# Soft-MoE over linear attention on one core: early loads joined, w loads reordered, one output chunk stored in uneven pieces

## The chip, the cores and the metric

The kernel runs on one core of a Trainium2 chip. The metric is the device time of one execution in microseconds. Before the change it is 172.59 us, the median of three runs (172.44 to 172.74).

## What is computed

The reference, cut to its core. q, k and v are 8 batches x 8 heads x 576 x 64 in float32; x has 4608 rows of 512; there are 8 experts of 4 slots, with w1 of 512 x 1024 and w2 of 1024 x 512 each.

```python
kv = np.einsum('bhsd,bhse->bhde', k, v)
out = np.einsum('bhsd,bhde->bhse', q, kv)
out = out / np.sqrt(np.mean(out * out, -1, keepdims=True) + 1e-06) * g_norm
x = out.transpose(0, 2, 1, 3).reshape(B * S, H * D)

logits = x @ phi
d = softmax(logits, axis=0)
slot_input = (d.T @ x).reshape(E, S_per_e, D)
for e in range(E):
    slot_out[e] = np.maximum(slot_input[e] @ w1[e], 0.0) @ w2[e]
c = softmax(logits, axis=1)
return c @ slot_out.reshape(n_slots, D)
```

## The kernel before

The kernel is written for five engines and records every instruction in an Order object, which then puts the semaphore waits in. All instructions are issued from its one line 204, so the rows of the profile are told apart by their tiles. The engines keep the order in which the code calls them.

The 4608 rows of x are worked on in 36 tiles of 128, T0 to T35; nine tiles belong to two batches. For each batch b, the class Kv makes the products of k and v (methods products and borders, 64x64 matmuls named "psum<-arena" in the trace), and slots turns them and writes them into a block matrix bds[b % 2] through ACT. The function products(T) then multiplies q by that matrix (matmuls "psum<-bd,arena", 128x192), with two PSUM tiles in turn; square(T) and evict(T) let ACT copy the result out, VectorE makes the mean squares, GpSimd scales. The table kv_steps (line 625) says behind which tile the steps 0, 1 and 2 of a batch stand: steps 0 and 1 are its products, step 2 is slots. Logits, a running maximum and the weighted sums of x by groups of six tiles follow along.

When all tiles are done, expert_h makes relu(slot_input @ w1) for eight experts, expert_y the products with w2 in two halves, combine the row softmax. gather and mix collect a half, and output(hf, k, f) makes one of twelve output chunks: matmuls "psum<-logits,part", then ACT and VectorE copy to the chunk's place in SBUF, of 128 partitions x 1536 floats (6144 B a partition).

All inputs, w and the outputs lie in one SBUF array, arena, of 160 KB a partition, whose regions are used again: KV_AT, Q_AT, W_AT and OUT_AT give the places. All DMAs go out on SyncE (SP) in program order, and one waits until the last reader of its place is done. The early loads (lines 320 to 327) go out at once: "first" (constants and half of kv of batch 0), the other half of kv0, q of batches 0 and 1, kv1 in two halves, the rest of q0, kv2, q1. kv3, kv4 and kv5 follow behind batch 0's products (lines 685 to 687); then loads_behind (line 330) issues one load behind each of the tiles 9, 18, 24 and 27, and load_w is called by hand further down. W_ROWS (line 40) says which units of w1 and w2 (16 KB a partition each, some in halves) one load takes; its order is also the order in DRAM.

OUT_ROWS (line 51) says which chunks a store takes: chunks 0 to 2, 3 to 5, 6 and 7, 8 to 11, each as one DMA of 128 rows once its last chunk is written:

```python
for row in OUT_ROWS:
    if row[-1] == n:
        nc.sync.dma_start(out[...].rearrange("o (p n) -> (o p) n", p=P), place(OUT_AT[row[0]], m))
```

Of the kernel before, what the change touches and what calls it, by code (L numbers as in the profile page):

```python
# [5 lines left out]
F32 = mybir.dt.float32  # L6
# [5 lines left out]
P = 128  # L12
# [15 lines left out]
TOK = 4608  # L28
# [4 lines left out]
KV_AT = (0, 36, 54, 0, 90, 126, 18, 54)  # L33
Q_AT = (18, 72, 108, 36)
# [4 lines left out]
}  # L39
W_ROWS = (  # L40
    (("w1", 0, None), ("w1", 1, None)),
    (("w1", 2, None), ("w1", 3, None)),
    (("w1", 4, None), ("w2", 2, 1), ("w2", 0, None), ("w2", 1, None)),
    (("w2", 2, 0), ("w1", 6, None), ("w1", 5, None)),
    (("w1", 7, None),),
    (("w2", 3, None), ("w2", 4, None)),
    (("w2", 5, None), ("w2", 6, None)),
# [1 line left out]
)  # L49
OUT_AT = (32, 38, 44, 104, 110, 116, 122, 128, 134, 140, 146, 152)  # L50
OUT_ROWS = ((0, 1, 2), (3, 4, 5), (6, 7), (8, 9, 10, 11))
SHARED = (5, 11)
HEAD = 144
SCRATCH = 1024
# [206 lines left out]
def row_length(row):  # L261
    return sum(UNIT if part is None else UNIT // 2 for _, _, part in row)


def soft_moe_linear_attention(nc, first_in, kv_in, q0_in, q1_in, kv4_in, kv5_in, t3_in, w_in, out):


    const = Const(nc)
# [9 lines left out]
    def place(at, n):  # L278
        return arena[:, HEAD + at * KB : HEAD + at * KB + n]

    def load_row(at, src):
        nc.sync.dma_start(place(at, src.shape[-1]), src)
# [14 lines left out]
    def homes(kind, u):  # L297
        at = W_AT[kind, u]
        if at is None:
            return [xflat[:, :UNIT]]  # L300
        return [place(a, UNIT // len(at)) for a in at]

    def load_w(kind, u, part=None):
        i = [row[0] for row in W_ROWS].index((kind, u, part))
        lo = sum(row_length(row) for row in W_ROWS[:i])
        n = row_length(W_ROWS[i])
        src = w_in[:, lo * P : (lo + n) * P].rearrange("o (p n) -> (o p) n", p=P)
        t = homes(kind, u)[part or 0]
        if n > t.shape[-1]:
            t = place(W_AT[kind, u][part or 0], n)  # L310
        nc.sync.dma_start(t, src)

    def w_block(kind, u, i):
# [4 lines left out]


    nc.sync.dma_start(arena[:, : HEAD + 2304], first_in)  # L320
    load_row(KV_AT[0] + 9, kv_in[0, :, 2304:])
    load_row(Q_AT[0], q0_in[:, :2048])
    load_row(KV_AT[1], kv_in[1, :, :2304])
    load_row(KV_AT[1] + 9, kv_in[1, :, 2304:])
    load_row(Q_AT[0] + 8, q0_in[:, 2048:])
    load_row(KV_AT[2], kv_in[2])
    load_row(Q_AT[1], q1_in)


    loads_behind = {  # L330
        9: lambda: load_row(KV_AT[6], t3_in),
        18: lambda: load_w("w1", 0),
        24: lambda: load_w("w1", 2),
        27: lambda: load_w("w1", 4),
    }

    nc.scalar.preload_act_table_set("natural_log_exp_and_others")
# [4 lines left out]
    nc.gpsimd.memset(ones, 1.0)  # L342
    zeros = const.tile([P, 256], BF16, name="zeros")
    nc.vector.memset(zeros, 0.0)
    eps = const.tile([P, 1], F32, name="eps")
    nc.gpsimd.memset(eps, EPS_RMS)
    sel32 = const.tile([P, NS], F32, name="sel32")
# [5 lines left out]
    for i in range(2):  # L353
        lo = 64 * i
# [22 lines left out]
    class Kv:  # L377
# [10 lines left out]
        def products(self, r):  # L388
            g, w = divmod(r, 2)
            main = kv_main(self.b, g).rearrange("p (r w c n) -> p r w c n", r=2, w=2, c=4)  # L390
            for c in range(4):
                for i in range(2):
                    lo = 64 * i
                    nc.tensor.matmul(
                        self.pkv[lo : lo + 64, w, g],
                        lhsT=main[:, w, 1, c, lo : lo + 64],
                        rhs=main[:, w, 0, c, lo : lo + 64],
                        start=c == 0 and (g == 0 or self.b == 0),
                        stop=False,
                    )  # L400
# [222 lines left out]
    first = {b: 9 * (b // 2) + 4 * (b % 2) for b in range(B)}  # L623
    kvs = {}
    kv_steps = {(b, i - 3): (i,) for b in range(2, B) for i in range(3)}
    kv_steps.update({(1, -2): (0,), (1, -1): (1, 2)})
    kv_steps.update({(6, i - 4): (i,) for i in range(3)})
    del kv_steps[6, -1]

# [12 lines left out]
    ends = {starts[s + 1] - 1: s for s in range(len(STAGES))}  # L642
# [7 lines left out]
    def fill(n, cols=256, home=None):  # L650

        if not n:
            return
        t = home if home is not None else ps.tile([P, 2, 512], F32, tag="o", name="fill", bufs=2)[:, 1]
        for i in range(n):
            nc.tensor.matmul(
                t[:, :cols].rearrange("p (a n) -> p a n", n=256),
                lhsT=zeros[:, :P],
                rhs=zeros.unsqueeze(1).to_broadcast([P, cols // 256, 256]),
                start=True,  # L660
                stop=True,
            )
# [14 lines left out]
    for g in range(2):  # L677
        kv = Kv(0, "o" if g else "kv", 2 if g else None)
# [3 lines left out]
        fill(1, cols=512)  # L682
        kv.slots((g,))
        fill(EARLY[1 + g], cols=512)
    load_row(KV_AT[3], kv_in[3])
    load_row(Q_AT[1] + 8, kv4_in)
    load_row(Q_AT[2], kv5_in)
    T_at, diag_at, pb_at, d_at, sums_at = {}, {}, {}, {}, {}
    for T in range(NT - 2):
# [3 lines left out]
        o = products(T)  # L693
# [137 lines left out]
    def expert_h(e):  # L831
        ph = ps.tile([P, 2, 512], F32, tag="m", name=f"ph{e}")[:, 0, :256]
        for c in range(4):
            for j in range(4):
                nc.tensor.matmul(
                    ph[32 * j : 32 * j + 32],
                    lhsT=sTe[:, (4 * e + c) * NS : (4 * e + c + 1) * NS],
                    rhs=w_block("w1", e, 4 * c + j),
                    start=c == 0,
                    stop=c == 3,  # L840
                )
        h = wk.tile([P, 256], F32, tag="part", name=f"h{e}", bufs=3)
        nc.scalar.activation(h, ph, AF.Relu, scale=rs)

        x = xts[(NT - 1 - e // 2) % NX].rearrange("p j n -> p (j n)")
        hTs[e] = x[:, e % 2 * 256 : e % 2 * 256 + 256].rearrange("p (c n) -> p c n", n=NS)
        nc.vector.transpose(out=hTs[e].rearrange("p c n -> p (c n)"), in_=h)
# [28 lines left out]
    def mix(hf):  # L876
# [2 lines left out]
            nc.tensor.matmul(pz[f], lhsT=sel.rearrange("p a n -> p (a n)"), rhs=ys[hf][f], start=True, stop=True)  # L879
        zs[hf] = halves(f"z{hf}", pz)  # L880

    def output(hf, k, f):
        z = zs[hf]
        n = (hf * NCH + k) * 2 + f
        at = OUT_AT[n]
        st = place(at, 4 * CT * NS).rearrange("p (a n) -> p a n", a=4)
        shared = n in SHARED
        for v in range(2):
            fourth = hf == 1 and (2 * n + v) % 4 == 3
            apart = shared and v == 1  # L890
            pots = [
                ps.tile([P, 2, 512], F32, tag="y" if y else "m", name=f"po{hf}_{k}_{f}_{v}_{i}", bufs=1 if y else None)
                for i, y in enumerate((False, fourth) if apart else (fourth,))
            ]
            for u in range(2):
                lo = 32 * (2 * v + u)
                po = pots[u if apart else 0]
                nc.tensor.matmul(
                    po[:, 0 if apart else u, : CT * NS].rearrange("p (g x) -> p g x", g=2),
                    lhsT=z[f][lo : lo + 32],  # L900
                    rhs=cT[k][lo : lo + 32],
                    start=True,
                    stop=True,
                )
            if apart:
                nc.vector.tensor_copy(out=st[:, 2], in_=pots[0][:, 0, : CT * NS])
                nc.scalar.copy(st[:, 3], pots[1][:, 0, : CT * NS])
            elif v == 0:
                nc.scalar.copy(st[:, 0:2], pots[0][:, :, : CT * NS])
            else:  # L910
                nc.vector.tensor_copy(out=st[:, 2:4], in_=pots[0][:, :, : CT * NS])
        for row in OUT_ROWS:
            if row[-1] == n:
                lo, m = row[0] * 4 * CT * NS, len(row) * 4 * CT * NS
                nc.sync.dma_start(
                    out[:, lo * P : (lo + m) * P].rearrange("o (p n) -> (o p) n", p=P), place(OUT_AT[row[0]], m)
                )

    expert_h(0)
    expert_h(1)  # L920
    load_w("w2", 3)
# [20 lines left out]
    chunks = [(k, f) for k in range(NCH) for f in range(2)]  # L942
# [20 lines left out]
def build_program():  # L963
    import concourse.bacc as bacc

    nc = bacc.Bacc("TRN2", target_bir_lowering=False, num_devices=1, dynamic_dma_scratch_size=SCRATCH)
    shapes = {
        "first": (P, HEAD + 2304), "kv": (4, P, TOK), "q0": (P, TOK), "q1": (P, 2048),
        "kv4": (P, 2560 + TOK), "kv5": (P, 2 * TOK), "t3": (P, 3 * TOK),
        "w": (1, 2 * NE * P * UNIT),  # L970
    }
    args = [nc.dram_tensor(f"in_{n}_dram", s, F32, kind="ExternalInput").ap() for n, s in shapes.items()]
    args.append(nc.dram_tensor("out_0_dram", (1, 4 * NCH * P * 4 * CT * NS), F32, kind="ExternalOutput").ap())
    order = Order(nc)
    soft_moe_linear_attention(order, *args)
    order.emit()
    return nc
# [58 lines left out]
```

## Time and profile before

| | |
|---|---|
| median of three runs | 172.59 us |
| the profiled execution: its time | 172.53 us |
| its span, first to last instruction | 171.2 us |
| PE busy (matmul) | 149.1 us, 87% |
| ACT, DVE, POOL busy | 88.9, 86.0, 57.2 us |
| moved by DMA | 71.67 MB, mean 419 GB/s |
| data queue, share of 16 DMA engines | 97.6% |
| chain that ended last, by engine | PE 47%, DMA 26%, ACT 12%, DVE 5% |

The span is what the rows count from; the execution's own time is 1.3 us longer. The DMA share is the mean over the core's 16 DMA engines, and it counts a packet in the stretch in which it starts, so that short stretches can show more than 1. The instruction queues (q8 and q14) are fetches of code, which run on the same 16 engines as the data queue q1.

### The profile page before, as it was taken

The page shows a single profiled execution, that of the slowest core. Times are in us where ns is not written, and L with a number is a line of the kernel's source. Part 1 is how long each engine was busy: PE and PEld are TensorE (multiplying, and loading weights), DVE is VectorE, ACT ScalarE, POOL GpSimd, SP SyncE. Part 2 cuts the span into 40 slices and gives each one's busy share as a digit, 9 for nine tenths or more (in the row PEclk, how much of TensorE's full clock was granted, in tenths as well). Part 3 has the DMA queues.
Part 4 walks back from the last instruction along what each step waited for, and adds up shares of the span by engine and source line. Part 5 has one row for each costly group of instructions (what it writes and reads, how often), then busy time and mean ns, then how long its engine had stood idle before and what let it go on. Part 6 is the DMA issues. An engine that isn't in the chain of part 4 may idle for free.

```text
span 171.2 us, 4497 instructions
## 1 busy us (share of the span) xinstructions
PE 149.1 (87%) x1975; PEld 108.1 (63%) x1975; DVE 86.0 (50%) x184; ACT 88.9 (52%) x230; POOL 57.2 (33%) x68
## 2 busy tenths in 40 slices
PE   7787897989999899999899999999999988989400
PEld 3467776979688888898797775455565444445100
DVE  1122156283677265763936798724897027137400
ACT  2037576786965887768849864203213025137400
POOL 6000708548356755466482579200000000000000
PEclk9999999999999999999999999999999999999965
DMA  5999999999999999999999999998999999999995
GB/s 192 416 422 433 439 415 437 472 421 474 417 413 458 430 426 430 406 404 452 433 492 419 431 429 389 434 450 354 436 478 387 461 390 421 439 396 439 406 459 241
DMA packets 3476, 71.67 MB, mean 419 GB/s; under 512 B 384, under 2 KB 384, under 8 KB 384
## 3 DMA queue, kind: packets, MB, share of 16 engines
q1 hardware_dynamic: 3456, 71.38, 97.6%
q8 instruction: 15, 0.25, 0.5%
q14 instruction: 5, 0.04, 0.1%
HBM read 61.94 MB, written 9.44 MB: 417 GB/s over the span
## 4 chain that ended last, share of the span: by engine, by line
PE 47%; DMA 26%; ACT 12%; DVE 5%; SPq 2%; issue 1%
PE psum L204 47%; DMA arena<-in_kv_dram 13%; DMA arena<-in_w_dram 13%; ACT bd L204 3%; ACT sq L204 3%; ACT xall L204 2%; SPq L204 2%; DVE logits L204 1%; ACT arena L204 1%; DVE ms L204 1%; ACT part L204 1%; ACT d L204 1%; ACT r L204 1%; DVE r L204 0%; DVE d L204 0%
## 5 line engine op out<-in xcount | busy, mean ns | idle before, releaser
L204 PE MATMUL psum<-bd,arena 128*128 128x192 f32 (+1 forms) x320 | 56.1, 335 | 1.9 <-ACT bd L204 1.5
L204 PEld LDWEIGHTS psum<-bd,arena 128*128 128x128 f32 (+1 forms) x320 | 45.4, 179 | 7.1 <-ACT bd L204 2.8
L204 DVE TENSOR_REDUCE ms<-sq 128x16 f32<-128x1024 f32 (+1 forms) x19 | 22.1, 1162 | 32.6 <-ACT sq L204 32.3
L204 POOL TENSOR_TENSOR xall<-xall,r 128x512 f32<-128x512 f32 x34 | 34.8, 1044 | 0.0
L204 POOL TENSOR_TENSOR part<-part,r 128x512 f32<-128x512 f32 x17 | 17.8, 1049 | 49.7 <-DVE r L204 49.7
L204 ACT ACTIVATE sq<-psum 128x512 f32<-128x512 f32 x36 | 21.5, 598 | 12.6 <-PE psum L204 12.4
L204 PE MATMUL psum<-arena 128*64 128x64 f32 (+1 forms) x640 | 21.7, 226 | 3.3 <-DMA arena<-in_kv_dram 2.2
L204 PEld LDWEIGHTS psum<-arena 128*64 128x64 f32 (+1 forms) x640 | 19.0, 137 | 7.9 <-DMA arena<-in_kv_dram 3.5
L204 ACT COPY xall<-psum 128x512 f32<-128x512 f32 x34 | 20.6, 606 | 0.0
L204 ACT COPY part<-psum 128x256 f32<-128x256 f32 (+1 forms) x38 | 13.6, 359 | 9.9 <-DVE part L204 8.8
L204 DVE TENSOR_REDUCE logits<-part 128x64 f32<-128x512 f32 (+1 forms) x18 | 17.8, 991 | 0.0
L204 PE MATMUL psum<-arena,xall 128*32 128x256 f32 x256 | 15.0, 380 | 0.4 <-DMA arena<-in_w_dram 0.2
L204 DVE COPY arena<-psum 128x768 f32<-128x768 f32 (+1 forms) x12 | 10.4, 889 | 8.4 <-PE psum L204 8.4
L204 ACT COPY arena<-psum 128x768 f32<-128x768 f32 (+1 forms) x14 | 10.1, 755 | 8.3 <-PE psum L204 8.3
L204 PE MATMUL psum<-logits,part 32*128 32x384 f32 x96 | 12.8, 521 | 1.5 <-ACT arena L204 0.9
L204 PE MATMUL psum<-arena,sq 128*32 128x256 f32 x224 | 12.7, 379 | 0.2 <-DVE sq L204 0.2
L204 PEld LDWEIGHTS psum<-arena,xall 128*32 128x32 f32 x256 | 8.0, 110 | 7.3 <-DMA arena<-in_w_dram 1.8
L204 PE MATMUL psum<-xall,d 128*32 128x129 f32 x288 | 10.8, 278 | 0.9 <-ACT d L204 0.9
L204 ACT COPY bd<-psum 64x128 f32<-64x128 f32 (+1 forms) x32 | 9.9, 309 | 1.6 <-PE psum L204 1.4
L204 PEld LDWEIGHTS psum<-logits,part 32*128 32x128 f32 x96 | 6.1, 183 | 7.1 <-ACT arena L204 4.2
L204 PEld LDWEIGHTS psum<-arena,sq 128*32 128x32 f32 x224 | 7.2, 110 | 5.2 <-DVE sq L204 0.6
L204 PEld LDWEIGHTS psum<-xall,d 128*32 128x32 f32 x288 | 7.0, 109 | 4.1 <-ACT d L204 2.2
(74 smaller groups left out, 118.9 us busy)
## 6 DMA issues: line engine op xcount, KB each, us to landing
arena<-in_w_dram SPq DMA_DIRECT2D x4, 4096.0 KB, 19.9
arena<-in_w_dram SPq DMA_DIRECT2D x1, 7168.0 KB, 27.5
arena<-in_t_dram SPq DMA_DIRECT2D x1, 6912.0 KB, 36.1
arena<-in_w_dram SPq DMA_DIRECT2D x1, 5120.0 KB, 17.9
arena<-in_kv_dram SPq DMA_DIRECT2D x2, 2304.0 KB, 23.4
arena<-in_kv_dram SPq DMA_DIRECT2D x1, 4608.0 KB, 42.6
out_dram<-arena SPq DMA_DIRECT2D x2, 2304.0 KB, 9.6
arena<-in_kv_dram SPq DMA_DIRECT2D x1, 3584.0 KB, 32.2
```

The source lines that it names most:

```text
L204: inst = getattr(engine, method)(*args, **kwargs)
```

## The change

The change has five parts.

- Early loads: the second half of kv0 and the first part of q0 become one load, the two halves of kv1 one, kv2 and the first part of q1 one. Six DMAs become three; the order of the bytes stays as it was but for that.
- kv_steps: batch 1's step 0 moves behind one tile more, and so do batch 2's steps 0 and 1 (step 0 by one tile, beside step 1).
- W_ROWS and loads_behind: the loads behind tiles 18, 24, 27 and after the tiles become loads behind tiles 18, 21, 24, 27, 30 and after the tiles; ten DMAs of w in all take the place of eight.
- The store of chunks 0 to 2 is taken apart. The even partitions still go out with three chunks, the odd ones with chunks 1 and 2 (store_first). Chunk 0 of the 64 odd partitions goes out as soon as it is written, in four DMAs (store_apart, after the table APART), two from GpSimd and two from SP.
- step_over loads a few bytes from DRAM into a tile that nothing reads, with 7 and with 6 rows (STEPS), on GpSimd ahead of each of its two stores.

```diff
 W_ROWS = (
     (("w1", 0, None), ("w1", 1, None)),
+    (("w2", 0, None), ("w2", 1, None)),
     (("w1", 2, None), ("w1", 3, None)),
-    (("w1", 4, None), ("w2", 2, 1), ("w2", 0, None), ("w2", 1, None)),
-    (("w2", 2, 0), ("w1", 6, None), ("w1", 5, None)),
+    (("w1", 4, None), ("w2", 2, 1)),
+    (("w1", 5, None),),
+    (("w2", 2, 0), ("w1", 6, None)),
     (("w1", 7, None),),
...
+CHUNK = 4 * 12 * 32
+APART = (("gpsimd", 0, 26, 2, 1), ("gpsimd", 41, 11, 2, 2), ("sync", 26, 15, 5, 1), ("sync", 52, 12, 3, 1))
+STEPS = (7, 6)
...
-    load_row(KV_AT[0] + 9, kv_in[0, :, 2304:])
-    load_row(Q_AT[0], q0_in[:, :2048])
-    load_row(KV_AT[1], kv_in[1, :, :2304])
-    load_row(KV_AT[1] + 9, kv_in[1, :, 2304:])
-    load_row(Q_AT[0] + 8, q0_in[:, 2048:])
-    load_row(KV_AT[2], kv_in[2])
-    load_row(Q_AT[1], q1_in)
+    load_row(KV_AT[0] + 9, kq0_in)
+    load_row(KV_AT[1], kv1_in)
+    load_row(Q_AT[0] + 8, q0_in)
+    load_row(KV_AT[2], kq2_in)
...
         18: lambda: load_w("w1", 0),
+        21: lambda: load_w("w2", 0),
         24: lambda: load_w("w1", 2),
         27: lambda: load_w("w1", 4),
+        30: lambda: load_w("w1", 5),
...
-    kv_steps.update({(1, -2): (0,), (1, -1): (1, 2)})
+    kv_steps.update({(1, -1): (0, 1, 2)})
+    kv_steps.update({(2, -2): (0, 1), (2, -1): (2,)})
+    del kv_steps[2, -3]
...
+    def step_over(n):
+        ends = [x[:n, : 2 * w].rearrange("p (c n) -> p c n", c=2)[:, :, :4] for x, w in ((steps, 8), (first_in, 64))]
+        nc.gpsimd.dma_start(*ends)
+
+    def store_apart():
+        at = 0
+        for j, (engine, lo, n, a, c) in enumerate(APART):
+            src = place(OUT_AT[0], CHUNK)[2 * lo + 1 : 2 * (lo + n) : 2]
+            size = n * CHUNK
+            dst = out[:, at : at + size].rearrange("o (b a n) -> (o a) b n", a=a, n=CHUNK // c)
+            if c > 1:
+                src = src.rearrange("p (c n) -> p c n", c=c)
+            getattr(nc, engine).dma_start(dst, src)
+            at += size
+            if j == 0:
+                step_over(STEPS[1])
+
+    def store_first():
+        at = 64 * CHUNK
+        for i in range(2):
+            n = (3 - i) * CHUNK
+            nc.sync.dma_start(out[:, at : at + 64 * n].rearrange("o (m n) -> (o m) n", n=n), place(OUT_AT[i], n)[i::2])
+            at += 64 * n
...
+        if n == 0:
+            store_apart()
+        if n == 2:
+            store_first()
+        for row in OUT_ROWS[1:]:
...
+    step_over(STEPS[0])
     expert_h(0)
```

How the instructions move. First PE, from the tiles T5 to T9; "psum<-bd,arena 128x192 x4" is one tile's products, "psum<-arena 64x64" the products of k and v of batch 2 (x16 is step 0, x24 step 1). Before:

```order
L204 MATMUL psum<-bd,arena 128x192 x4
L204 MATMUL psum<-arena 64x64 x16
L204 MATMUL psum<-bd,arena 128x192 x4
L204 MATMUL psum<-arena 64x64 x24
L204 MATMUL psum<-bd,arena 128x192 x4
L204 MATMUL psum<-ident,kvT 128x128 x2
L204 MATMUL psum<-gphi,kvT 128x128 x2
L204 MATMUL psum<-bd,arena 128x192 x8
```

and now:

```order
L209 MATMUL psum<-bd,arena 128x192 x8
L209 MATMUL psum<-arena 64x64 x40
L209 MATMUL psum<-bd,arena 128x192 x4
L209 MATMUL psum<-ident,kvT 128x128 x2
L209 MATMUL psum<-gphi,kvT 128x128 x2
L209 MATMUL psum<-bd,arena 128x192 x8
```

T6's products now stand ahead of all of batch 2's, and T7's behind them.

Next SP, from the load of kv6, q3 and kv7 (in_t) to the first stores; the numbers are partitions (or rows) x floats. Before:

```order
L204 DMA arena<-in_t_dram 128x13824
L204 DMA arena<-in_w_dram 128x8192 x2
L204 DMA arena<-in_w_dram 128x14336
L204 DMA arena<-in_w_dram 128x10240
L204 DMA xall<-in_w_dram 128x4096
L204 DMA arena<-in_w_dram 128x8192 x2
L204 DMA arena<-in_w_dram 128x4096
L204 DMA out_dram<-arena 128x4608 x2
```

and now:

```order
L209 DMA arena<-in_t_dram 128x13824
L209 DMA arena<-in_w_dram 128x8192 x3
L209 DMA arena<-in_w_dram 128x6144
L209 DMA arena<-in_w_dram 128x4096
L209 DMA arena<-in_w_dram 128x6144
L209 DMA xall<-in_w_dram 128x4096
L209 DMA arena<-in_w_dram 128x8192 x2
L209 DMA arena<-in_w_dram 128x4096
L209 DMA out_dram<-arena 5x3x1536
L209 DMA out_dram<-arena 3x4x1536
L209 DMA out_dram<-arena 64x4608
L209 DMA out_dram<-arena 64x3072
```

The four loads between in_t and xall became six, none longer than 8192 floats a partition, and the first store became four on this queue.

Last POOL, at its end; before, nothing followed the last MEMSET (which clears the slot matrix sTe):

```order
L204 TENSOR_TENSOR part<-part 128x2x128
L204 TENSOR_TENSOR part<-part 128x2x64
L204 TENSOR_TENSOR logits<-part 128x64
L204 TENSOR_TENSOR xall<-xall,r 128x4x128 x2
L204 MEMSET sq 128x1024
```

and now:

```order
L209 MEMSET sq 128x1024
L209 DMA steps<-in_first_dram 7x2x4
L209 DMA out_dram<-arena 2x13x1536
L209 DMA steps<-in_first_dram 6x2x4
L209 DMA out_dram<-arena 2x11x768
```

Four DMAs are issued from POOL, which issued none; "2x13x1536" is 26 rows, "2x11x768" 11 rows in 22 halves.

## Rows read from the trace of the kernel before

**Rows 1.** The page: span, packets, and queues (packets, MB, share of 16 engines).

```profile
span 171.2 us, 4497 instructions
...
DMA packets 3476, 71.67 MB, mean 419 GB/s; under 512 B 384, under 2 KB 384, under 8 KB 384
...
q1 hardware_dynamic: 3456, 71.38, 97.6%
q8 instruction: 15, 0.25, 0.5%
q14 instruction: 5, 0.04, 0.1%
```

**Rows 2.** Table by stretches: length, busy by engine, PEclk, DMA share, GB/s.

```profile
1.50:2.00 0.50, 0.50 (x3) 0.22 (x2) 0.21 (x1) 0.50 (x1) 0.23 (x1) 1.00 1.11 157
4.00:150.00 146.00, 136.56 (x1883) 101.79 (x1881) 79.10 (x173) 81.05 (x219) 54.29 (x55) 1.00 1.00 429
```

**Rows 3.** The same table, short stretches of the tail.

```profile
151.50:152.00 0.50, 0.50 (x16) 0.30 (x12) 0.00 (x0) 0.04 (x1) 0.00 (x0) 1.00 0.35 147
161.50:162.00 0.50, 0.00 (x0) 0.00 (x0) 0.00 (x0) 0.00 (x0) 0.00 (x0) 1.00 0.64 270
162.00:162.25 0.25, 0.00 (x0) 0.00 (x0) 0.00 (x0) 0.00 (x0) 0.00 (x0) 1.00 2.16 934
163.00:163.25 0.25, 0.00 (x0) 0.00 (x0) 0.00 (x0) 0.00 (x0) 0.00 (x0) 1.00 0.47 197
163.25:163.50 0.25, 0.00 (x0) 0.00 (x0) 0.00 (x0) 0.00 (x0) 0.00 (x0) 1.00 1.15 492
168.00:168.50 0.50, 0.00 (x0) 0.00 (x0) 0.00 (x0) 0.00 (x0) 0.00 (x0) 0.50 1.03 442
169.00:169.50 0.50, 0.00 (x0) 0.00 (x0) 0.00 (x0) 0.00 (x0) 0.00 (x0) 0.50 0.12 49
169.50:170.00 0.50, 0.00 (x0) 0.00 (x0) 0.00 (x0) 0.00 (x0) 0.00 (x0) 0.50 0.68 295
```

**Rows 4.** Timeline of SP: issues of the second and last store (start, us).

```profile
151.57 0.34 SPq L204 DMA_DIRECT2D out_dram<-arena  x1
...
161.19 0.33 SPq L204 DMA_DIRECT2D out_dram<-arena  x1
```

**Rows 5.** The chain that ended last, in order of time: its DMA pieces.

```profile
3.82 22.84 DMA arena<-in_kv_dram
...
122.21 22.24 DMA arena<-in_w_dram
```

**Rows 6.** Timeline of PE, start and us, tiles T0 to T9.

```profile
11.86 2.87 PE L204 MATMUL psum<-bd,arena 128*128 128x192 f32 x16 [0.40 <-ACT bd L204]
...
20.95 4.47 PE L204 MATMUL psum<-bd,arena 128*128 128x192 f32 x32
26.70 1.15 PE L204 MATMUL psum<-arena 128*64 128x64 f32 x32 [1.28 <-DMA arena<-in_kv_dram]
27.78 1.57 PE L204 MATMUL psum<-bd,arena 128*128 128x192 f32 x8
29.28 1.54 PE L204 MATMUL psum<-arena 128*64 128x64 f32 x48
...
34.94 1.24 PE L204 MATMUL psum<-bd,arena 128*128 128x192 f32 x6 [0.65 <-ACT bd L204]
```

**Rows 7.** Timeline of PE in the tail.

```profile
132.44 1.98 PE L204 MATMUL psum<-ones 128*128 128x512 f32 x4
134.67 3.66 PE L204 MATMUL psum<-arena,xall 128*32 128x256 f32 x64 [0.25 <-DMA arena<-in_w_dram]
...
143.40 0.97 PE L204 MATMUL psum<-logits,part 32*128 32x384 f32 x8 [0.36 <-DVE arena L204]
144.49 3.66 PE L204 MATMUL psum<-arena,xall 128*32 128x256 f32 x64
...
150.95 1.29 PE L204 MATMUL psum<-arena,xall 128*32 128x256 f32 x20
```

More of the change, by code (lines that the diff above doesn't have):

```diff
@@ L262, in row_length, with apart_pieces, soft_moe_linear_attention @@
     return sum(UNIT if part is None else UNIT // 2 for _, _, part in row)
-def soft_moe_linear_attention(nc, first_in, kv_in, q0_in, q1_in, kv4_in, kv5_in, t3_in, w_in, out):
+def apart_pieces():
+    return [
+        np.array([(2 * m + 1, h, c) for m in range(lo, lo + n) for h in range(c)]).reshape(a, -1, 3).swapaxes(0, 1).reshape(-1, 3)
+        for _, lo, n, a, c in APART
+    ]
+def soft_moe_linear_attention(nc, first_in, kq0_in, kv1_in, q0_in, kq2_in, kv3_in, kv4_in, kv5_in, t3_in, w_in, out):
     const = Const(nc)
@@ L344, in soft_moe_linear_attention @@
     nc.vector.memset(zeros, 0.0)
+    steps = const.tile([P, 16], F32, name="steps")
     eps = const.tile([P, 1], F32, name="eps")
@@ L684, in soft_moe_linear_attention @@
         fill(EARLY[1 + g], cols=512)
-    load_row(KV_AT[3], kv_in[3])
+    load_row(KV_AT[3], kv3_in)
     load_row(Q_AT[1] + 8, kv4_in)
@@ L911, in output @@
                 nc.vector.tensor_copy(out=st[:, 2:4], in_=pots[0][:, :, : CT * NS])
-        for row in OUT_ROWS:
+        if n == 0:
[3 more added lines that the diff above has]
+        for row in OUT_ROWS[1:]:
             if row[-1] == n:
@@ L967, in build_program @@
     shapes = {
-        "first": (P, HEAD + 2304), "kv": (4, P, TOK), "q0": (P, TOK), "q1": (P, 2048),
+        "first": (P, HEAD + 2304), "kq0": (P, 2304 + 2048), "kv1": (P, TOK), "q0": (P, 2560),
+        "kq2": (P, TOK + 2048), "kv3": (P, TOK),
         "kv4": (P, 2560 + TOK), "kv5": (P, 2 * TOK), "t3": (P, 3 * TOK),
@@ L1017 @@
         "in_first_dram": first,
-        "in_kv_dram": kv[:4],
-        "in_q0_dram": qm[0],
-        "in_q1_dram": np.ascontiguousarray(qm[1][:, :2048]),
+        "in_kq0_dram": np.concatenate([kv[0][:, 2304:], qm[0][:, :2048]], axis=1),
+        "in_kv1_dram": kv[1],
+        "in_q0_dram": np.ascontiguousarray(qm[0][:, 2048:]),
+        "in_kq2_dram": np.concatenate([kv[2], qm[1][:, :2048]], axis=1),
+        "in_kv3_dram": kv[3],
         "in_kv4_dram": np.concatenate([qm[1][:, 2048:], kv[4]], axis=1),
@@ L1029 @@
     n = 4 * CT * NS
-    chunks = []
-    for row in OUT_ROWS:
+    three = np.empty((P, 3 * n), np.float32)
+    at = 0
+    for pieces in apart_pieces():
+        for p, h, c in pieces:
+            w = n // c
+            three[p, h * w : h * w + w] = res[0, at : at + w]
+            at += w
+    three[::2] = res[0, at : at + 192 * n].reshape(64, 3 * n)
+    three[1::2, n:] = res[0, at + 192 * n : 3 * P * n].reshape(64, 2 * n)
+    chunks = [three[:, k * n : k * n + n] for k in range(3)]
+    for row in OUT_ROWS[1:]:
         part = res[0, row[0] * n * P : (row[-1] + 1) * n * P].reshape(P, len(row), n)
```

## The prediction, made before the changed kernel was run

> **What bounds the kernel now.** I read the page's totals first. In [rows 1] the data queue keeps 16 DMA engines busy for 97.6% of the 171.2 us span, with 71.38 MB. A mean over the span can hide stages, so the next view is the table by stretches: from 4 to 150 us the DMA share is 1.00 at 429 GB/s [rows 2], which is 429/16 = 26.8 GB/s for one engine. No transfer is waiting to be issued in that time; bytes set the pace. The first packets start at 1.5 to 2.0 us [rows 2]. If all engines had equal work, they would end near 1.75 + 0.982 x 171.2 = 169.9 us (97.6 + 0.5 + 0.1% of [rows 1]).
>
> They don't end together. The last store moves 128 rows of 24,576 B, eight an engine, and the view counts a packet in the stretch where it starts. Bytes of a stretch over 24,576 B give the number of packets: 442 GB/s x 0.5 us = 221 KB is nine packets from 168.0 to 168.5, where the early engines start their last one, and 49 and 295 GB/s are one and six packets from 169.0 to 170.0 [rows 3]. So **nine engines end about 1.2 us before the other seven**. One packet takes 24,576 B / 26.8 = 0.914 us, and the last of them, begun at some 169.78, ends near 170.7. The same split shows where that store begins: a burst of nine at 162.0 to 162.25, then two and five at 163.0 to 163.5 [rows 3]. The nine began together because they had waited for its issue at 161.19 [rows 4]: 161.5 to 162.0 shows a share of 0.64. After the issue at 151.57 the same is seen at 151.5 to 152.0, with 0.35 [rows 3]. Those two holes are (0.65 + 0.36) x 0.5 x 16 = 8.1 engine-us, 0.9 us for each of nine. Their true lead is therefore about 1.2 + 0.9 = 2.1 us.
>
> Beside the queue stands compute, and the chain of waits shows how close it is: it names a landing of kv that ends at 26.66 us and then none until a load of w issued at 122.21 [rows 5]. Compute sets when the last store can be issued.
>
> **The change, part by part.** *The uneven store.* Of the first three output chunks, chunk 0 of the 64 odd partitions (64 pieces of 6,144 B, four an engine in an even deal, 0.229 us each) leaves the common store. The numbers are 26 rows as 2 x 13, 15 as 5 x 3, 12 as 3 x 4, and 11 rows in 22 halves (a third place of the order, below "the change"). Dealt by the leading index, two engines get 13, one gets 11, three get 3 + 4 = 7, two get 3 and eight get none (26 + 11 + 21 + 6 = 64). The eight save 4 x 0.229 = **0.92 us**; the two take on 9 x 0.229 = 2.06 us, the one 1.60, the three 0.69. The nine lead by 2.1 us on average, so there is room for the 2.06 if it goes to the foremost. How a DMA of two leading entries is dealt no row shows. That each row stays a packet, and each DMA closes on all 16, is all that [rows 1] tell: 3,456 packets are 24 DMAs x (128 + 16), and the 384 under 512 B are 24 x 16. The bounds are an even deal (gain 0) and a deal by leading index to early engines (gain 0.92). I take the second, since rows dealt evenly would need each piece cut, and 128-row stores show no cut. [...]
>
> The dummy loads of 7 and 6 rows and the descriptors run on POOL, whose last instruction was a MEMSET ahead of the experts, so nothing queues behind them; by the rows of a packet 16 bytes cost nothing, and if each cost a whole small piece (0.229) on six or seven engines, the loss is at most 0.2. I take 0. The pieces from POOL may be served between those of the last w load on three early engines, and delay its landing there by up to 2.06 us; these engines are ahead by that much, and the matmuls that read it come late (150.95, [rows 7]). Cost 0; with a later w landing it would move the tail one for one.
>
> *The joined early loads.* Bytes do not change. Three issues fewer at SP save some 0.4 us of SP each, with a full queue behind: 0. But two loads now land with a companion: kv0's second half with 1.05 MB of q0, and kv2 with 1.05 MB of q1. At 429 GB/s each is **2.44 us later**. PE waited for both: T0's products, behind batch 0's second half, start at 11.86, and kv2's at 26.70 after 1.28 us of waiting [rows 6]. So T0 starts near 14.3 and kv2 near 29.1.
>
> *Two batches a tile later.* This decides what that lateness costs. Before, T6 (1.50 us at 27.78) stood behind the first kv2 step; now it stands ahead of it, so it fills the wait. T3 to T5 ended at 25.42 [rows 6]; all shifted by 2.44, they end at 27.86 and T6 at 29.4. From kv2's start to T9's took 34.94 - 26.70 = 8.24; without T6, 6.74. T9 now starts between 29.1 + 6.74 = 35.84 and 29.4 + 6.74 = 36.1, 0.9 to 1.2 us late. I take 0.9: the 29.4 shifts all of T0 to T5 in full, and part of their time was a wait for kv1, whose landing stays. Batch 1's steps are moved alike, and its load lands with the same bytes ahead of it: 0 beyond the shift.
>
> From there the chain has no DMA wait to absorb anything until 134.42, when PE's filler ends and w is 0.25 us away [rows 7]. So 0.9 becomes 0.65 at 134.67. At 144.49 PE waits again, after ending at 144.37; 0.12 goes, and **0.53 us** is left for the last store's issue: 161.72, its first packets at 162.55 (0.83 behind the issue, as in [rows 3, 4]).
>
> *The w loads.* Same bytes in eight to ten DMAs; the w2 pair comes three tiles earlier, w1 unit 5 before the last pair. SP issues sooner, and a queue that was never empty gains nothing: 0. Two more sets of 16 small packets: 0. It costs if a buffer is not yet free, and then w1 unit 6 lands late next; each load stands behind the tile that frees its place.
>
> **The sum**, against the profiled execution of 172.53 us (span 171.2 and 1.3 around it; 0.06 under the median of 172.59). The late engines now begin the last store near 170.7 - 8 x 0.914 = 163.39. Shedding 0.92 puts that at 162.47, and compute lets it begin at 162.55. So 0.84 of the 0.92 is realised: 172.53 - 0.84 = 171.69, **171.7 us**. Leveling alone gives 170.7 - 169.9 = 0.8, the same size. Its own range is 171.1 (holes also filled, no lateness) to 172.1 (an engine of the eight still 0.4 behind).
>
> **The rivals.** *Compute overtakes the queue* (slower). If the whole 2.44 us passes to T9, the last store's issue moves by 2.44 - 0.25 - 0.12 = 2.07, its packets begin at 162.02 + 2.07 = 164.09, 0.70 after the late engines' 163.39 of now: 173.2 us. It decides from 163.39 - 162.02 = 1.37 us at the store, 1.74 us at T9. For it: the chain has no slack from 26.7 to 122 us [rows 5]. Against it: T6 fills 1.50 of the wait.
>
> *The pieces fall on wrong engines* (slower). One that is late and gets 13 pieces ends 2.06 us later: 174.6 us. It takes only one of the three big shares on the seven. The trace does not number engines, which is for it; against it, three shares of 13, 13 and 11 fit a lead of about 2 us. [...]
>
> *The deal is even* (no change). Then the seven stay late and 0.53 us of compute lateness hides under their 1.37: 172.5 us. For it: every DMA of the trace closes on 16 engines.
>
> **How the numbers follow.** A difference under 0.2% (0.35 us) can't be told from none. Forecast 0.70, even deal 0.12, compute overtakes 0.10, wrong engines 0.08. Below 172.24: nearly all of the forecast and a bit of the even deal, 0.70; within: 0.13; above 172.94: 0.17. The range has to hold forecast and even deal, 0.82, and so runs from 171.0, a little under the forecast's own low end, to 172.7.
>
> **What would show it.** Right: the last packets start within some 0.9 us of each other; no holes near 152 and 162; T9 near 35.8; the last store issued near 161.7. Wrong: T9 after 36.7, a last issue after 162.6, the two clusters of last packets still 1.2 us apart, or two or three lone packets at the very end.

## The result, and the profile after

The changed kernel takes **173.53 us** (median of 22 runs, 172.38 to 174.87), the kernel before 172.56 us (22 runs, 172.42 to 172.97). The ratio is 1.006 (95% interval 1.0044 to 1.0076): slower, where 171.7 us was forecast, and outside the range. The spread is as telling as the median, 2.5 us where it was 0.55. The profiled execution is the slowest of the 22, 174.87 us. Two executions far from all others, 438.77 us of the kernel before and 293.08 us of "Other engines" below, stand outside every comparison.

The page of it, span, granted TensorE clock in 40 slices, data queues and the chain that ended last by engine:

```profile
span 173.6 us, 4508 instructions
...
PEclk9985899999999999999999999999999999999955
...
q1 hardware_dynamic: 3363, 71.15, 96.2%
q0 software_dynamic: 480, 0.23, 0.5%
...
PE 65%; ACT 15%; DVE 7%; DMA 6%; issue 1%; SPq 0%
```

In both kernels the chain ends with the last copy ahead of the last store. DMA was 26% of it and is 6%, all of it the wait for the joined load in_kq at its start; behind that, compute runs through to the last store without a wait for a load. And the clock, which was 1.00 from 4 to 150 us ([rows 2]), shows 8, 5, 8 tenths in the slices from 8.7 to 21.7 us. The table by stretches (columns as in [rows 2]) says what was ahead of that:

```profile
6.00:8.70 2.70, 2.61 (x46) 1.70 (x45) 0.76 (x3) 0.67 (x3) 0.00 (x0) 1.00 1.01 432
8.70:11.40 2.70, 0.01 (x1) 0.01 (x2) 0.25 (x2) 0.12 (x1) 0.00 (x0) 1.00 1.00 429
11.40:20.00 8.60, 8.41 (x64) 7.53 (x65) 0.44 (x2) 2.46 (x7) 0.00 (x0) 0.60 1.02 433
```

PE did nothing for 2.7 us, and behind that its granted clock was 0.60 on average over 8.6 us, and 0.50 from 12.5 to 18.75 us. The timeline of PE: first two lines of before that [rows 6] leaves out, the last filler and batch 0's second half, which follow each other with 0.13 us between:

```profile
8.59 0.38 PE L204 MATMUL psum<-zeros 128*128 128x512 bf16 x1
9.10 1.43 PE L204 MATMUL psum<-arena 128*64 128x64 f32 x40
```

and then the changed kernel, the answer to [rows 6]:

```profile
11.39 1.84 PE L209 MATMUL psum<-arena 128*64 128x64 f32 x40 [2.71 <-DMA arena<-in_kq_dram]
...
14.72 6.22 PE L209 MATMUL psum<-bd,arena 128*128 128x192 f32 x24 [0.19 <-ACT bd L209]
...
29.79 1.57 PE L209 MATMUL psum<-bd,arena 128*128 128x192 f32 x8 [0.76 <-ACT xall L209]
31.29 2.48 PE L209 MATMUL psum<-arena 128*64 128x64 f32 x80
...
37.88 1.57 PE L209 MATMUL psum<-bd,arena 128*128 128x192 f32 x8 [0.64 <-ACT bd L209]
```

Batch 0's second half starts at 11.39 instead of 9.10, after a wait that was not there before. T0 to T2 take 6.22 us, and T9 starts at 37.88 instead of 34.94: **2.94 us late**, not 0.9. kv2 shows no wait for its load any more; the tiles ahead of it were what came late. In the tail, SP's issue of the last store (it was at 161.19, [rows 4]) and then the stretches in which last packets start ([rows 3]; 49 GB/s in half a microsecond is one packet of 24,576 B, 737 are fifteen):

```profile
163.58 0.33 SPq L209 DMA_DIRECT2D out_dram<-arena  x1
```

```profile
170.50:171.00 0.50, 0.00 (x0) 0.00 (x0) 0.00 (x0) 0.00 (x0) 0.00 (x0) 0.50 1.71 737
171.00:171.50 0.50, 0.00 (x0) 0.00 (x0) 0.00 (x0) 0.00 (x0) 0.00 (x0) 0.50 0.11 49
171.50:172.00 0.50, 0.00 (x0) 0.00 (x0) 0.00 (x0) 0.00 (x0) 0.00 (x0) 0.50 0.13 49
172.00:172.50 0.50, 0.00 (x0) 0.00 (x0) 0.00 (x0) 0.00 (x0) 0.00 (x0) 0.50 0.11 49
```

The last store is issued 2.39 us later, past the 1.37 us from which compute was to decide. And three lone packets, of two engines (a packet takes 0.91 us), come behind the rest, and the last of them ends some 1.2 us after it; the prediction named such packets at the very end as a sign that it is wrong. So there were two things to tell apart: the clock, and the store.

The runs themselves sort by mean granted clock. Five runs of 0.976 to 0.979 took 172.38 to 173.21 us (median 172.97), eight of 0.963 to 0.970 took 172.78 to 173.71, nine of 0.954 to 0.960 took 173.99 to 174.87.

### The profile page after: what moved, and what is told of

It is laid out like the page before. It is cut to its first block, busy times and chain, and to the rows that moved or that the text cites. A ratio compares the mean times of both kernels' runs of the same rounds, so it can differ in the third digit from the quotient of the medians.

```text
span 173.6 us, 4508 instructions
## 1 busy us (share of the span) xinstructions
PE 152.0 (88%) x1975; PEld 110.9 (64%) x1975; DVE 86.0 (50%) x184; ACT 88.7 (51%) x230; POOL 59.9 (35%) x72
## 3 DMA queue, kind: packets, MB, share of 16 engines
q1 hardware_dynamic: 3363, 71.15, 96.2%
## 4 chain that ended last, share of the span: by engine, by line
PE 65%; ACT 15%; DVE 7%; DMA 6%; issue 1%; SPq 0%
PE psum L209 65%; DMA arena<-in_kq_dram 6%; ACT bd L209 4%; ACT sq L209 3%; ACT xall L209 2%; DVE ms L209 2%; ACT arena L209 2%; DVE logits L209 1%; ACT part L209 1%; ACT r L209 1%; DVE arena L209 1%; ACT d L209 1%; DVE part L209 1%; DVE r L209 0%; DVE d L209 0%
## 5 line engine op out<-in xcount | busy, mean ns | idle before, releaser
L209 PE MATMUL psum<-bd,arena 128*128 128x192 f32 (+1 forms) x320 | 57.9, 343 | 2.5 <-ACT bd L209 1.3
L209 PEld LDWEIGHTS psum<-bd,arena 128*128 128x128 f32 (+1 forms) x320 | 47.5, 185 | 7.9 <-ACT bd L209 2.7
L209 ACT ACTIVATE sq<-psum 128x512 f32<-128x512 f32 x36 | 21.5, 597 | 12.5 <-PE psum L209 12.4
L209 POOL DMA_DIRECT2D out_dram<-arena x2 | 1.5, 730 | 33.0 <-ACT arena L209 33.0
```

Source lines behind the costliest of these rows:

```text
L209: inst = getattr(engine, method)(*args, **kwargs)
```

## The experiments

The change has three parts that can be put in alone: J (joined loads with the moved kv_steps), W (the w order) and S (the uneven store). All were timed in five rounds against the kernel before (172.5 to 172.6 us).

**Fillers in the wait (J, W, S).**

```diff
-EARLY = (5, 1, 0)
+EARLY = (5, 12, 0)
```

EARLY counts fillers, matmuls of the tile zeros whose results nothing reads.

> The changed kernel with eleven more filler matmuls behind batch 0's first half, where PE stood idle from 8.7 to 11.4 us. Theory 'clock' (the wait for the joined load lets the granted clock fall to 0.5 for some 7 us, and that makes compute late): the clock stays at 1.00 up to the tail, T9's products start near 35.8 us instead of 37.9, and the time is the forecast one, 171.7 us (171.3 to 172.2), with the spread of 2.5 us between runs gone. Theory 'store' (the uneven pieces leave one or two engines late, whatever compute does): no better than the changed kernel's runs of the highest mean clock (0.976 to 0.979), 172.4 to 173.2 us, with one or two lone packets at the end.

172.65 us (172.31 to 174.15). The clock stays at 1.00 up to the tail, T0 starts at 14.19 and T9 at 35.69, where 35.84 was forecast. The clock theory is right about its half, and 0.9 us comes back; but the time is no better than before, and a spread of 1.8 us stays. So the store theory holds as well.

**Old early loads (W, S)**: the seven load_row lines and the kv_steps of before.

> The changed kernel with the early loads and kv_steps of before; the w loads and the uneven store stay. Theory 'clock': T9 at 34.9 us, no fall of the clock, 171.6 us (171.2 to 172.1). Theory 'store': 172.4 us or more, for the same engines stay late.

172.18 us (171.95 to 173.06), ratio 0.9988 (0.9976 to 1.0000). About 0.3 us is gained in the median, under half of the 0.84 and hardly clear of the noise, with a spread of 1.1 us; both theories missed in part.

**Joined loads alone (J).**

> The kernel before with the joined early loads and the moved kv_steps alone; w loads and store as before. Theory 'clock': this part alone brings the loss and the spread, 173 to 174.5 us, with T9 near 37.9 us where the clock fell. Theory 'store': the late compute hides under the late engines, 172.5 us (172.2 to 172.9).

174.43 us (172.73 to 175.24, six runs), as the clock theory had it. In its profile (174.17 us) the clock fell for a shorter time, 0.80 on average from 11.4 to 20 us against 0.60, and T9 started at 36.53; so the fall is not all of this loss.

**Fillers, even store (J, W)**: the first kernel of this list with the store of before.

> As the filled kernel (eleven more fillers, joined loads, new w order), but with the even store of before. The difference to the filled kernel is the worth of the uneven store alone. Theory 'clock': 172.4 to 172.6 us, 0.8 us more than the filled one. Theory 'store': the same as or less than the filled one.

172.47 us (172.28 to 172.73), and tight. With the fillers in, the uneven store wins nothing in the median (172.65, a difference of 0.2 us, too small to be told from none) and brings the long runs.

**W alone**, and **S alone**:

> The kernel before with the new order of the w loads alone (loads behind tiles 18, 21, 24, 27, 30). Theory 'clock and store': the queue was never empty, so 172.5 us, no difference to before (172.3 to 172.7). Rival 'w order': the 0.3 us that old loads with the new w order and the uneven store gained come from here, 172.2 us.

> The kernel before with the uneven store alone. Theory 'clock and store': the store is worth 0.3 us with old loads and brings the spread, 172.2 us with runs from 171.9 to 173.1, the ten latest engines within 0.6 us of each other. Rival 'w order': 172.5 us or more.

W alone is 172.62 us (172.56 to 172.83): nothing, as forecast. S alone is 172.56 us (172.08 to 173.02): no gain in the median, and the spread. Its profiled run, of 172.89 us, in the stretches where last packets start:

```profile
169.00:169.50 0.50, 0.00 (x0) 0.00 (x0) 0.00 (x0) 0.00 (x0) 0.00 (x0) 0.50 0.46 197
169.50:170.00 0.50, 0.00 (x0) 0.00 (x0) 0.00 (x0) 0.00 (x0) 0.00 (x0) 0.50 0.01 0
170.00:170.50 0.50, 0.00 (x0) 0.00 (x0) 0.00 (x0) 0.00 (x0) 0.00 (x0) 0.50 0.12 49
```

The group of seven at the end is gone ([rows 3] showed 49 and 295 from 169.0 to 170.0). In its place four packets start by 169.5, and **one engine alone** starts its last after 170.0.

**kq0 apart** (J without its first join, W, S):

```diff
-    load_row(KV_AT[0] + 9, kq0_in)
+    load_row(KV_AT[0] + 9, kq0_in[:, :2304])
+    load_row(Q_AT[0], kq0_in[:, 2304:])
```

> The changed kernel with one of the three joined loads taken apart again: kv0's second half and q0's first part are two DMAs, all else stays. Theory 'clock': PE's wait at 8.7 to 11.4 us is gone, the clock stays at 1.00, T0's products start at 11.9 us, T9's at 35.0 to 35.7, and the time is 172.1 to 172.5 us without runs over 173.5. Rival 'any joined load' (the late kv2 is enough to make compute late): T9 after 37 us, 173 us or more.

172.73 us (171.87 to 174.23). In the profiled run T0 starts at 11.98, T0 to T2 take 4.58 us as with the fillers, and the mean clock is 0.976 (0.958 in the profiled run of the changed kernel), so the fall in the traces hangs on this one join. It is not shown for every run: the one of 174.23 us has a mean clock of 0.961, where the filled kernel's eleven have 0.974 to 0.981. T9 still starts at 35.89, behind waits of 1.78 us for kv1 and 0.49 us for kv2, and long runs remain: time and spread were forecast too small.

**Other engines** (W, S): dummy loads of 11 and 2 rows.

```diff
-STEPS = (7, 6)
+STEPS = (11, 2)
```

> The kernel with old early loads, new w order and uneven store, but dummy loads of 11 and 2 rows instead of 7 and 6. Theory 'pieces go to named engines by the rows of the dummy loads': the two shares of 13 fall on other engines, of which most are late ones, so one or two engines end up to 2 us after the rest: 173.0 to 174.5 us. Rival 'the deal does not depend on the dummy loads': 172.2 us as with 7 and 6.

174.78 us, three runs within 0.03 us (174.75 to 174.78). Last packets:

```profile
169.00:169.50 0.50, 0.00 (x0) 0.00 (x0) 0.00 (x0) 0.00 (x0) 0.00 (x0) 0.50 0.46 197
169.50:170.00 0.50, 0.00 (x0) 0.00 (x0) 0.00 (x0) 0.00 (x0) 0.00 (x0) 0.50 0.01 0
171.00:171.50 0.50, 0.00 (x0) 0.00 (x0) 0.00 (x0) 0.00 (x0) 0.00 (x0) 0.50 0.23 98
171.50:172.00 0.50, 0.00 (x0) 0.00 (x0) 0.00 (x0) 0.00 (x0) 0.00 (x0) 0.50 0.23 98
```

Fourteen engines have begun their last packet by 169.5, exactly two start theirs after 171.5 (98 GB/s are two packets). The two shares of 13 go to two engines, which two depends on the dummy loads, and on these two they cost 2.6 us against 7 and 6 rows (172.18). That the three runs agree so closely speaks for the same two engines in each; one of them has a trace.

**J and W with the even store, no fillers**, and **J with fillers and the old w order**, which fill the table of J, W and fillers:

> Joined early loads, moved kv_steps and new w order, even store, no added fillers. Theory 'the clock fall is the loss' : as the filled kernel with the even store (172.47) plus what the fall costs; with T9 1 to 2 us later than 35.7 and the last store issued near 162.5 to 163.6, 173.0 to 174.3 us with a spread of over 1 us. Rival 'the loss needs the old w order too' (joined loads alone lost 1.9 us because late compute left the queue empty): 172.4 to 172.7 us.

> Joined early loads and moved kv_steps with eleven more fillers, old w order, even store. Theory 'the clock fall is the loss': clock 1.00, T9 at 35.7, 172.5 us (172.3 to 172.8). Rival 'the loss needs the old w order too': the loads behind the tiles are issued 0.8 us later than before, the queue runs empty once, 172.8 to 173.4 us.

J and W: 173.12 us, in two heaps, six runs from 172.41 to 172.62 and six from 173.62 to 174.16. The mean granted clock divides them in the same way, 0.978 to 0.979 in the lower heap and 0.955 to 0.961 in the upper. The profiled run is of the upper heap (173.63 us). Its table, its PE and SP timelines and last packets:

```profile
8.70:11.40 2.70, 0.12 (x3) 0.09 (x4) 0.29 (x2) 0.15 (x1) 0.00 (x0) 1.00 0.98 421
11.40:20.00 8.60, 8.41 (x64) 7.53 (x65) 0.44 (x2) 2.56 (x7) 0.00 (x0) 0.60 1.02 434
```

```profile
14.81 6.03 PE L206 MATMUL psum<-bd,arena 128*128 128x192 f32 x24 [0.19 <-ACT bd L206]
...
37.77 1.57 PE L206 MATMUL psum<-bd,arena 128*128 128x192 f32 x8 [0.65 <-ACT bd L206]
```

```profile
163.53 0.33 SPq L206 DMA_DIRECT2D out_dram<-arena  x1
```

```profile
170.50:171.00 0.50, 0.00 (x0) 0.00 (x0) 0.00 (x0) 0.00 (x0) 0.00 (x0) 0.50 1.82 786
171.00:171.50 0.50, 0.00 (x0) 0.00 (x0) 0.00 (x0) 0.00 (x0) 0.00 (x0) 0.50 0.00 0
```

All sixteen engines start their last packet together (786 GB/s are sixteen), since all have waited for the store: here compute alone sets the end. The same kernel with fillers, table and timelines:

```profile
8.70:11.40 2.70, 2.52 (x15) 0.99 (x13) 0.30 (x2) 0.17 (x1) 0.00 (x0) 1.00 1.05 448
11.40:20.00 8.60, 8.00 (x116) 6.86 (x118) 2.17 (x6) 4.56 (x13) 0.00 (x0) 1.00 0.99 420
```

```profile
14.05 4.58 PE L206 MATMUL psum<-bd,arena 128*128 128x192 f32 x24 [0.40 <-ACT bd L206]
...
35.70 1.57 PE L206 MATMUL psum<-bd,arena 128*128 128x192 f32 x8 [0.64 <-ACT bd L206]
```

```profile
161.41 0.33 SPq L206 DMA_DIRECT2D out_dram<-arena  x1
```

With PE busy from 8.7 to 11.4 the clock is 1.00, T0 to T2 take 4.58 us instead of 6.03, T9 starts 2.07 us earlier and the last store is issued 2.12 us earlier. The upper heap has its median at 173.70 us, the lower at 172.48, the filled kernel at 172.47. So the price of the fall is 1.2 us of time, and it comes or not from run to run.

J with fillers and the old w order: 173.08 us (172.60 to 174.08), the rival's range. The new order is worth 0.6 us beside J (173.08 to 172.47), and more without fillers (174.43 to 173.12). The table from 75 to 120 us, joined loads alone, and then joined loads with the new order:

```profile
75.00:120.00 45.00, 42.92 (x567) 31.66 (x571) 28.87 (x67) 25.98 (x74) 22.60 (x24) 1.00 0.99 411
```

```profile
75.00:120.00 45.00, 42.91 (x552) 32.09 (x554) 28.04 (x66) 26.09 (x75) 23.74 (x25) 1.00 1.00 427
```

411 against 427 GB/s over 45 us are 0.7 MB that came later (the kernel before has 426): with late compute, the old order issues the loads behind the tiles too late to keep the queue full. With fillers the hole is smaller and lies in one place: the load that went out at 102.38 us before goes out at 103.00, and the DMA share from 104 to 105 us is 0.27 (before: 0.82).

**Softer shares** (W, S), in two steps, by the author's count 8 and 6 pieces over the even four for the two big shares:

```diff
-APART = (("gpsimd", 0, 26, 2, 1), ("gpsimd", 41, 11, 2, 2), ("sync", 26, 15, 5, 1), ("sync", 52, 12, 3, 1))
+APART = (("gpsimd", 0, 22, 2, 1), ("gpsimd", 42, 9, 2, 2), ("sync", 22, 20, 5, 1), ("sync", 51, 13, 13, 1))
...
+APART = (("gpsimd", 0, 16, 2, 1), ("gpsimd", 31, 7, 2, 2), ("sync", 16, 15, 5, 1), ("sync", 38, 26, 13, 1))
```

> Old early loads, new w order, and the uneven store with softer shares: 22 rows on two engines, 9 in halves on one, 20 on five, 13 rows one each on thirteen. The late engines shed 3 of 4 pieces (0.69 us), the two big shares are 8 over the even four instead of 9. Theory 'single engines with a big share set the end': about as the kernel with the full shares, 172.0 to 172.2 us, runs within 0.9 us. Rival 'what is shed is not won': 172.4 to 172.6 us.

> The same with shares softer still: 16 rows on two engines, 7 in halves on one, 15 on five, 26 rows two each on thirteen. Late engines shed 2 of 4 pieces (0.46 us), the two big shares are 6 over the even four. Theory 'single engines with a big share set the end': no engine passes the late ones any more, 172.1 us (172.0 to 172.3) with runs within 0.5 us. Rival 'what is shed is not won': 172.4 to 172.6 us.

172.52 us (172.12 to 173.10) and 172.31 us (172.24 to 172.42, ratio 0.9982, 0.9974 to 0.9991). The softest shares win a little, in every run (before: 172.42 to 172.84); the softer ones still spread, as the full size did.

**Two big shares, one big share** (W, S): first 24 rows for two shares of 12, and no share of 11; then the share of 11 alone, behind a dummy load of 15 rows. The other rows go out from SP:

```diff
+APART = (("gpsimd", 0, 24, 2, 1), ("sync", 24, 15, 5, 1), ("sync", 39, 12, 3, 1), ("sync", 51, 13, 13, 1))
+STEPS = (7, 7)
...
+APART = (("gpsimd", 0, 11, 2, 2), ("sync", 11, 15, 5, 1), ("sync", 26, 12, 3, 1), ("sync", 38, 26, 13, 1))
+STEPS = (15, 16)
```

> [...] Theory 'the third engine (11 rows) is the one that falls behind in some runs': tight runs within 0.5 us, near 172.0. Theory 'one of the two': the spread of 1 us stays, 172.0 to 173.1. If any engine with a big share can be hit: both kernels spread, this one more.

> [...] Theory 'the third engine falls behind in some runs': the spread of 1 us stays, 172.1 to 173.1. Theory 'one of the two': tight runs within 0.5 us, 172.1 to 172.3.

**172.16 us** (171.96 to 172.37, ratio 0.9976, 0.9967 to 0.9985) and 172.37 us (172.19 to 172.59). With two shares the spread is gone, though each is 12 rows, and 13 pieces if one of the single rows falls to it: it goes with the third share. But the third share alone doesn't bring the spread back, so its 11 pieces aren't enough by themselves; what they meet in the full version stays open. The kernel with two shares beats the kernel before by 0.4 us, and the changed one. Its last packets:

```profile
168.00:168.50 0.50, 0.00 (x0) 0.00 (x0) 0.00 (x0) 0.00 (x0) 0.00 (x0) 0.50 1.25 541
168.50:169.00 0.50, 0.00 (x0) 0.00 (x0) 0.00 (x0) 0.00 (x0) 0.00 (x0) 0.50 0.91 393
169.00:169.50 0.50, 0.00 (x0) 0.00 (x0) 0.00 (x0) 0.00 (x0) 0.00 (x0) 0.50 0.46 197
169.50:170.00 0.50, 0.00 (x0) 0.00 (x0) 0.00 (x0) 0.00 (x0) 0.00 (x0) 0.50 0.01 0
```

The packets' sizes in the traces say a little more. Pieces of 6,144 B that start as late as 152 to 155 us: three in the traced run of S alone, three with the softer shares, four with the fillers, four with kq0 apart and eight with 11 and 2 rows; none with old early loads (172.13 us), the softest shares, two shares and one share. So in these traces an engine that ends after the others goes with pieces that are late, which points to an engine with a big share; the views don't number engines, so this is argued and not shown. The changed kernel has no such pieces, though two of its engines end late: its stores are issued late, and engines that wait for them lose the lead that was to cover a big share. That too is argued.

## Why the prediction was wrong

**The early loads and the kv step: the step that failed.** "T9 now starts between 29.1 + 6.74 = 35.84 and 29.4 + 6.74 = 36.1, 0.9 to 1.2 us late." It started 2.94 us late, at 37.88. The lateness of the loads was right, and so was the working from kv2's start to T9: with fillers T9 starts at 35.69 and 35.70. What was left out is what the wait does to PE itself. "PE waited for both" is a wrong reading for the first of the two loads: before, PE began batch 0's second half 0.13 us behind a filler, with no wait. So the 2.44 us by which it lands later became a new gap in PE's work, and the prediction took the tiles behind it at their old durations. But an idle PE of 2.6 to 2.7 us was followed by a granted clock of 0.60 on average from 11.4 to 20 us (the changed kernel, and J and W without fillers; 1.00 with them), which costs 2.1 us at T9 and 2.1 us at the last store (J and W with and without fillers). The prediction did not weigh it.

**The rival came true by another road.** Compute overtook the queue, at 173.2 us by the forecast, because "the whole 2.44 us passes". The upper heap of J and W lies at 173.6. The threshold was right: 1.37 us at the store, and it was 2.34 there; the 0.97 us above it would give 173.5. The chance of 0.10 was too small, since only one source of lateness was in it.

**"0.84 of the 0.92 is realised."** No run shows the deal that the 0.92 and the 2.06 are added up from (two engines with 13, one with 11, three with 7, two with 3, eight with none), for the views don't number engines. What the runs showed fits it: 3,363 packets of q1 in the changed kernel are 2,971 rows and 392 small ones, 16 for each of 24 DMAs, and five and three for the stores of 5 x 3 and 3 x 4 rows; with dummy loads of 11 and 2 rows two engines end late; and in S alone the group of seven at the end is gone. But S alone won nothing, W and S 0.3 us, and two shares 0.4. The sum took the nine early engines by their mean lead of 2.1 us and gave three of them nearly all of it. It named "wrong engines" as a fixed thing, and did not ask what happens if in some runs one of the loaded engines has less lead. Then one engine sets the end where seven had shared it, and the slack of the mean is of no use. The trace shows one engine that ends alone (one lone packet in S alone). That it is a loaded one is argued, and what delays it was not shown.

Two smaller terms of the same sum were off. The small packets were taken at 0: S alone has 852 packets under 512 B (384 before), and the times of all packets over 16 engines add up to 168.5 us against 168.2, so that 0.3 us of what levelling can give goes to more work. And the joined loads were to cost 0.08 us beside the uneven store; with the clock full they cost 0.5 in the median (172.65 against 172.18), though nothing beside the even one (172.47 against 172.62).

**The w loads at 0**: right without the joined loads (172.62), wrong beside them. "A queue that was never empty gains nothing" holds while compute is on time; with compute late it was worth 0.6 us and more.

Put together, J and W cost 0.5 us in the median (173.12), nearly all of which the fillers give back (172.47), and S another 0.4 on top (173.53). The first of these medians lies between two heaps, so these two steps are rough.

## What to carry to other kernels

Where a change makes PE wait longer, its price may be more than the wait (here 0.60 of the clock for 8.6 us behind 2.7 us of it): look at the granted clock behind such waits, and put work or fillers there before anything else is judged. A load levelled over the DMA engines is only as good as its most unlucky engine (here two of sixteen, with dummy loads of 11 and 2 rows, which began their last packets after 171.5 us where the others had by 169.5), so shares should stop short of the measured lead. A change that brings in spread has to be read by its heaps, for a median between two of them names neither.

## What the runs showed of the hardware

The same kernel falls to a lower clock in some runs and not in others, by the mean granted clock of each: six of twelve for J and W, with 0.955 to 0.961 against 0.978 to 0.979. The traces are of runs that fell, after waits of 2.56 to 2.71 us; the wait in the others was not traced. The GpSimd store of 2 x 13 rows went to two engines (two packets in each of the last stretches with 11 and 2 rows), and which two could be set by dummy DMAs of 7 or 11 rows ahead of it (172.18 and 174.78 us). Which engines these are no run shows: the views don't number engines.
